# The last copy out of PSUM and the output's store on ScalarE, in a gated attention/gMLP decode kernel

## The chip, the cores and the metric

The kernel runs on one core of one Trainium2 chip. The metric is the device time of one execution in microseconds, as the median over several executions. The profile's "span" is about 1.9 us shorter than that time (385.2 against 387.0 us for the profiled execution of the kernel before) and moves with it.

## The reference

One token (batch 1, sequence 1, width 1024) goes through two branches that a sigmoid gate mixes. Branch A is attention with 32 query heads over 4 cached key/value heads of 65,536 positions; branch B is a small gMLP block. Cut to what matters:

```python
g = sigmoid((x * gate_w).sum(-1, keepdims=True))
q = (x @ wq)                                    # 32 heads of 128
p = softmax(q @ repeat(k_cache, 8).T * 128**-0.5)
a = (p @ repeat(v_cache, 8)) @ wo               # out: (1, 1, 1024), bfloat16
b = gmlp(x, w_in, w_sp, b_sp, w_out)
return g * a + (1 - g) * b
```

The caches and weights are 162 MB, the output is 2 KB.

## The kernel before

SyncE issues all large loads in program order into a ring of four 4 MB buffers. At the very end the output projection accumulates into one tile `out_ps` in PSUM, the memory that the matmuls write to; it has 128 partitions by 256 float32 columns, in which four groups of 32 equal rows hold the four quarters of the output. The last weight, `wo`, comes in ever smaller chunks, so that little work remains after the last of them. Then one copy casts the PSUM tile to bfloat16, and one DMA stores four of its rows, 512 B each.

```python
WO_SPLIT = ((16,), (8, 4, 2, 1, 1))
# ... loads, queries, 4 heads of scores, softmax and values: cut ...
    wo_view = A_wo.rearrange("(p c) n -> p c n", c=OC)
    c0 = 0
    for split in WO_SPLIT:
        t = kv.tile([P, CT * P], BF16, name="wo_t", tag="kv")
        t = t[:].rearrange("p (c n) -> p c n", n=D)
        b = c0
        for n in split:
            nc.sync.dma_start(out=t[:, c0 - b:c0 - b + n, :], in_=wo_view[:, c0:c0 + n, :])  # L417
            project(t[:, c0 - b:c0 - b + n, :], n, oa, c0, last=(c0 + n == OC))      # matmuls, L382
            c0 += n
    out_sb = const.tile([P, NO], BF16, name="out_sb")
    nc.vector.tensor_copy(out=out_sb[:], in_=out_ps[:])                              # L421
    nc.sync.dma_start(out=out.rearrange("o t (q n) -> (o t q) n", n=NO), in_=out_sb[::B, :])  # L422
```

## Time and profile before

| | before |
|---|---|
| time, median of 3 (range) | 386.87 us (386.82 to 386.92) |
| span of the profiled execution | 385.2 us |
| read from HBM | 162.01 MB, 421 GB/s over the span |
| from the end of the last matmul to the end of the span | 3.00 us |

Lines of the page of the kernel before. PE is TensorE and PEld its weight loads, DVE is VectorE, ACT ScalarE, POOL GpSimd. First the title and the busy time of each engine with its share of the span; then the share of busy time in 40 equal slices, in tenths, for ScalarE (ACT) and for the DMA engines; then the DMA queues with packets, MB and share of the 16 engines' time; last the chain that ended last, by engine.

```profile
span 385.2 us, 3265 instructions
PE 212.4 (55%) x1396; PEld 89.7 (23%) x1396; DVE 209.2 (54%) x207; ACT 39.2 (10%) x54; POOL 4.4 (1%) x10
...
ACT  1010001111601101014011010140110101400000
...
DMA  8999999999999999999999999999999999999993
...
q1 hardware_dynamic: 6200, 162.01, 98.1%
...
q10 hardware_dynamic: 36, 0.00, 0.0%
...
DMA 65%; DVE 18%; PE 9%; issue 5%; ACT 1%; SPq 0%; ACTq 0%; DVEq 0%
```

The DMA row stands at 9 from the second slice to the last but one, and SyncE's load queue q1 is busy for 98.1% of the span: the kernel is bound by its input stream. No compute engine is over 55%. At the end only the last slice (3) falls off: in it lies the tail, by which I mean the stretch from the end of the last matmul to the end of the span. ScalarE has nothing in the last five slices. Its queue q10 carries only 36 packets, the four tiny loads at the start.

The tail itself, as the timeline of the kernel before from 381 us (start, length, engine, line, operation, and in brackets how long the engine was idle and what ended it; SPq is SyncE's issuing of a DMA):

```profile
381.12 0.29 PE L382 MATMUL out_ps<-wo_t,oa 128*32 128x256 bf16 x4 [0.25 <-DMA wo_t<-in_A_wo_dram]
...
381.76 0.41 PE L382 MATMUL out_ps<-wo_t,oa 128*32 128x256 bf16 x4 [0.35 <-DMA wo_t<-in_A_wo_dram]
...
382.22 0.42 DVE L421 CAST out_sb<-out_ps 128x256 bf16<-128x256 f32 x1 [12.43 <-PE out_ps L382]
382.67 0.66 SPq L422 DMA_DIRECT2D out_dram<-out_sb  x1
```

Read it as a staircase: each step starts where the one above it ends. The last chunk releases the last four matmuls at 381.76, they release the copy at 382.22, the copy releases the store's issue at 382.67, which ends at 383.33. The rest up to 385.17 is the store's flight (until its data packets move), its landing, and the closing steps of the program. Nothing else is going on, so all of this should be on the critical path; the 32 copies below test it.

What SyncE itself waits for at the end (longest in total first: waiter, what released it, total us, times, longest):

```profile
SPq L422 <- DVE out_sb L421: 30.3, 1, 30.3
...
SPq L457 <- DMA out_dram<-out_sb: 0.7, 1, 0.7
```

With its last load issued, it waited for VectorE's copy for the last 30.3 us before the store; no load is queued behind the store. L457 is the program's close, whose last wait is for the store's landing.

### The profile page before, as it was taken

The page shows a single profiled execution, that of the slowest core. Times are in us where ns is not written, and L with a number is a line of the kernel's source. Part 1 is how long each engine was busy: PE and PEld are TensorE (multiplying, and loading weights), DVE is VectorE, ACT ScalarE, POOL GpSimd, SP SyncE. Part 2 cuts the span into 40 slices and gives each one's busy share as a digit, 9 for nine tenths or more (in the row PEclk, how much of TensorE's full clock was granted, in tenths as well). Part 3 has the DMA queues.
Part 4 walks back from the last instruction along what each step waited for, and adds up shares of the span by engine and source line. Part 5 has one row for each costly group of instructions (what it writes and reads, how often), then busy time and mean ns, then how long its engine had stood idle before and what let it go on. Part 6 is the DMA issues. An engine that isn't in the chain of part 4 may idle for free.

```text
span 385.2 us, 3265 instructions
## 1 busy us (share of the span) xinstructions
PE 212.4 (55%) x1396; PEld 89.7 (23%) x1396; DVE 209.2 (54%) x207; ACT 39.2 (10%) x54; POOL 4.4 (1%) x10
## 2 busy tenths in 40 slices
PE   0433447775377656464876474637773837663352
PEld 0111113232222212122322121222221312331141
DVE  5141288996697372757864636569646456510010
ACT  1010001111601101014011010140110101400000
POOL 4000000000000000000000000000000000000000
PEclk9966559999779969695699695977895958565558
DMA  8999999999999999999999999999999999999993
GB/s 334 429 436 434 436 433 432 436 431 435 432 429 427 429 419 434 432 432 436 434 436 429 434 429 433 422 436 427 425 432 430 436 436 436 427 429 430 427 408 149
DMA packets 6251, 162.23 MB, mean 421 GB/s; under 512 B 728, under 2 KB 732, under 8 KB 1116
## 3 DMA queue, kind: packets, MB, share of 16 engines
q1 hardware_dynamic: 6200, 162.01, 98.1%
q8 instruction: 11, 0.18, 0.2%
q14 instruction: 4, 0.03, 0.0%
q10 hardware_dynamic: 36, 0.00, 0.0%
HBM read 162.01 MB, written 0.00 MB: 421 GB/s over the span
## 4 chain that ended last, share of the span: by engine, by line
DMA 65%; DVE 18%; PE 9%; issue 5%; ACT 1%; SPq 0%; ACTq 0%; DVEq 0%
DMA kn<-in_A_k_cache_dram 44%; DVE kt L295 15%; DMA vt<-in_A_v_cache_dram 9%; DMA wo_t<-in_A_wo_dram 9%; PE s_ps L301 6%; DMA wb<-in_B_b_sp_dram 2%; DVE pt L335 1%; PE o_ps L344 1%; PE z_ps L190 1%; ACT sc L310 1%; PE om_ps L355 0%; SPq L417 0%; ACT sc L332 0%; DVE mx L314 0%; DVE mx L297 0%
## 5 line engine op out<-in xcount | busy, mean ns | idle before, releaser
L301 PE MATMUL s_ps<-kt,wt 128*128 128x512 bf16 x512 | 139.0, 426 | 88.4 <-DVE kt L295 87.2
L295 DVE STREAM_TRANSPOSE kt<-kn 128x2048 int32<-128x2048 int32 x64 | 143.3, 2283 | 68.4 <-DMA kn<-in_A_k_cache_dram 68.4
L301 PEld LDWEIGHTS <-wt 128*128 128x128 bf16 x512 | 52.6, 105 | 173.5 <-DVE kt L295 72.8
L344 PE MATMUL o_ps<-vt,pt 128*32 128x512 bf16 x512 | 39.4, 457 | 15.4 <-DMA vt<-in_A_v_cache_dram 15.4
L310 ACT CAST sc<-s_ps 128x1024 bf16<-128x1024 f32 x16 | 16.2, 1013 | 254.9 <-PE s_ps L301 254.9
L344 PEld LDWEIGHTS <-pt 128*32 128x32 bf16 x512 | 15.9, 109 | 34.9 <-issue 27.1
L335 DVE STREAM_TRANSPOSE pt<-sc 128x1024 bf16<-128x1024 bf16 x16 | 18.6, 1217 | 6.8 <-ACT sc L332 6.8
L332 ACT ACTIVATE sc<-sc,nb 128x1024 bf16<-128x1024 bf16 x16 | 18.2, 1136 | 9.5 <-DVE nb L328 9.5
L352 DVE COPY o_sb<-o_ps 128x512 f32<-128x512 f32 x4 | 2.6, 662 | 27.2 <-PE o_ps L344 27.2
L297 DVE TENSOR_REDUCE mx<-sc 128x1 f32<-128x1024 bf16 x12 | 14.3, 1188 | 1.2 <-ACT sc L310 1.1
L355 PE MATMUL om_ps<-o_sb,pick 128*32 128x128 f32 x32 | 7.7, 421 | 13.1 <-DVE o_sb L352 13.1
L190 PE MATMUL q_ps<-wq_t,xT 128*32 128x512 bf16 x64 | 7.1, 623 | 9.1 <-DMA wq_t<-in_A_wq_dram 9.1
L314 DVE TENSOR_REDUCE mx<-sc 128x1 f32<-128x1024 bf16 x4 | 4.9, 1220 | 12.3 <-ACT sc L310 12.3
L382 PE MATMUL out_ps<-wo_t,oa 128*32 128x256 bf16 x128 | 6.0, 334 | 7.7 <-DMA wo_t<-in_A_wo_dram 7.7
L190 PEld LDWEIGHTS <-xT 128*32 128x32 bf16 x128 | 5.2, 140 | 20.5 <-issue 20.5
L355 PEld LDWEIGHTS om_ps<-o_sb,pick 128*32 128x32 f32 x32 | 5.0, 168 | 17.2 <-DVE o_sb L352 16.3
L254 DVE TENSOR_TENSOR rowt<-q_ps,own_b 128x512 f32<-128x512 f32 x2 | 1.3, 685 | 14.1 <-PE q_ps L190 14.1
L190 PE MATMUL z_ps<-win_t,xT 128*32 128x448 bf16 x64 | 6.2, 567 | 4.8 <-DMA win_t<-in_B_w_in_dram 4.8
L421 DVE CAST out_sb<-out_ps 128x256 bf16<-128x256 f32 x1 | 0.4, 425 | 12.4 <-PE out_ps L382 12.4
L318 PE MATMUL mt_ps<-ident_f,m 128*1 128x128 f32 x4 | 1.2, 296 | 10.2 <-DVE m L316 10.2
L382 PEld LDWEIGHTS <-oa 128*32 128x32 bf16 x128 | 4.4, 116 | 9.1 <-issue 7.2
L202 DVE TENSOR_TENSOR rowt<-z_ps,own_b 128x448 f32<-128x448 f32 x2 | 1.2, 620 | 9.3 <-PE z_ps L190 9.3
(86 smaller groups left out, 57.4 us busy)
## 6 DMA issues: line engine op xcount, KB each, us to landing
kn<-in_A_k_cache_dram SPq DMA_DIRECT2D x16, 4096.0 KB, 27.1
vt<-in_A_v_cache_dram SPq DMA_DIRECT2D x16, 4096.0 KB, 34.6
wq_t<-in_A_wq_dram SPq DMA_DIRECT2D x2, 4096.0 KB, 28.3
win_t<-in_B_w_in_dram SPq DMA_DIRECT2D x2, 3584.0 KB, 15.0
wo_t<-in_A_wo_dram SPq DMA_DIRECT2D x1, 4096.0 KB, 31.1
wout_t<-in_B_w_out_dram SPq DMA_DIRECT2D x1, 3584.0 KB
wo_t<-in_A_wo_dram SPq DMA_DIRECT2D x1, 2048.0 KB
wo_t<-in_A_wo_dram SPq DMA_DIRECT2D x1, 1024.0 KB
```

The source lines that it names most:

```text
L190: nc.tensor.matmul(ps[t * B:(t + 1) * B, k * HN:k * HN + n], lhsT=xT[:, i * KH + c:i * KH + c + 1].to_broadcast([P, B]), rhs=w[:, c, o:o + ...
L295: nc.vector.transpose(out=kt[:].bitcast(I32), in_=kb[:, v * n:(v + 1) * n])
L297: nc.vector.reduce_max(**late.pop())
L301: nc.tensor.matmul(s_ps[:, k * HN:(k + 1) * HN], lhsT=wt[g % 2][:, v, b].rearrange("p a v h -> p (a v h)"), rhs=kx[:, b // 2, b % 2, k * C ...
L310: nc.scalar.copy(out=sct[g, j][:], in_=s_ps[:])
L314: nc.vector.reduce_max(**late.pop())
L332: nc.scalar.activation(out=sct[g, j][:], in_=sct[g, j][:], func=ACT.Exp, scale=SCALE, bias=nb[:, 0:1], accum_out=lss[g][:, j:j + 1])
L335: nc.vector.transpose(out=ptt[g, j][:].rearrange("p c x -> p (c x)"), in_=sct[g, j][:])
L344: nc.tensor.matmul(o_ps[g][t * B:(t + 1) * B, :], lhsT=ptt[g, j][:, c, :], rhs=vx[:, c], start=(j == 0 and c < NB), stop=(j == NT - 1 and ...
L352: nc.vector.tensor_copy(out=o_sb[:], in_=o_ps[g][:])
L355: nc.tensor.matmul(om_ps[gs, :], lhsT=pick[:, i * REP:(i + 1) * REP, :].rearrange("p h q -> p (h q)"), rhs=o_sb[:, i * DH:(i + 1) * DH], s ...
L382: nc.tensor.matmul(out_ps[t * B:(t + 1) * B, :], lhsT=vec[:, c0 + c:c0 + c + 1].to_broadcast([P, B]), rhs=w[:, c, t * NO:(t + 1) * NO], st ...
```

## The change

The intent is to have one engine do copy and store, without a hand-over from VectorE to SyncE, on ScalarE, which is idle at the end.

```diff
     out_sb = const.tile([P, NO], BF16, name="out_sb")
-    nc.vector.tensor_copy(out=out_sb[:], in_=out_ps[:])
-    nc.sync.dma_start(out=out.rearrange("o t (q n) -> (o t q) n", n=NO), in_=out_sb[::B, :])
+    nc.scalar.copy(out=out_sb[:], in_=out_ps[:])
+    nc.scalar.dma_start(out=out.rearrange("o t (q n) -> (o t q) n", n=NO), in_=out_sb[::B, :])
```

## The prediction

> **What bounds the kernel now.** The input stream. The page gives 162.01 MB read at 421 GB/s over a span of 385.2 us, the load queue busy 98.1% of the span, and the DMA row at 9 in all slices but the first and last. The chain that ended last is 65% DMA; VectorE's 18% and TensorE's 9% of it are the handshakes inside that stream. The change edits only the tail behind the last weight chunk, which is wholly on the critical path.
>
> **The tail before** (timeline from 381 us, span's clock): the last wo_t chunk lands at 381.72; the last out_ps matmuls end near 382.19; VectorE's copy L421 starts about 0.05 us later and takes 0.425 us; SyncE starts issuing the store about 0.03 us after its end, at 382.67, and takes 0.66 us; the rest up to 385.2 (1.84 us) is the store's flight, its landing and the closing barrier.
>
> **What changes.** In instruction order one copy leaves VectorE, one DMA leaves SyncE, and both stand at the end of ScalarE's list; nothing else moves. No activation-table load is added: the op is the same plain copy as the L310 casts, which run between exponentials without a reload.
>
> Term by term:
> 1. Start of the copy after TensorE: L310 casts on ScalarE start 0.036 us after the last matmul's end, L421 on VectorE 0.048 us after it: -0.01 us.
> 2. The copy: L310 takes 1013 ns for 1024 columns. With the 0.833 ns per element of the Trainium skill's "ScalarE: Activation LUTs" (What ACT_TABLE_LOAD costs), 256 columns make an estimated 1013 - 768 x 0.833 = 373 ns, against 425 ns on VectorE: -0.05 us.
> 3. Copy to issue: 0.03 us across engines now. On ScalarE the DMA is still made to wait for the copy's semaphore, so I expect 0.03 to 0.1 us: 0 to +0.07 us.
> 4. The issue itself: the store takes 658 ns on SyncE, where the loads take 328 to 437 ns. ScalarE's four issues at the start took 593, 283, 277 and 274 ns; the first looks cold. ScalarE's next DMA comes 380 us later: cold again, 0.55 to 0.75 us; 0.3 us would be the lucky case: about 0 us, -0.35 at best.
> 5. Flight and landing: unchanged. The Trainium skill's "DMA: Bandwidth & Descriptors" (Issuing engines are not separate DMA queues) says that transfers from either engine end on the same 16 DMA engines, and that another issuer saves only sequencer time. The load queue is empty by then, so there is nothing to overtake: 0.
> 6. VectorE and SyncE are freed of work, but only after everything else: worth nothing. SyncE's last closing wait is still for this store.
>
> **Sum:** -0.06 us, with -0.4 to +0.3 as the plausible spread, on 386.87. Predicted 386.8 us, 8 in 10 between 386.4 and 387.2. This is "same": 98%; faster by 2% would need 7.7 us, more than the whole tail of 3.4 us.
>
> **What would show it.** Everything up to 382.2 us agrees between the profiles; L421 is on ACT at about 0.37 us; the store stands under ACTq with 0.55 to 0.75 us, and its 4 data packets of 512 B on q10 instead of q1; no added ACT_TABLE_LOAD; VectorE's instruction count falls by one.
>
> **What would make it wrong.** A table load before the copy (+1.28 us, as at the start); a wake-up or cold fetch of ScalarE after 50 us without work; a slower issue for stores on ScalarE; or another chip or clock state shifting both kernels by more than the edit.

## The result and the profile after

| | before | after |
|---|---|---|
| time, median of 4 | 386.89 us (386.82 to 387.11) | 387.04 us (386.67 to 387.11) |
| ratio after/before | | 1.0001, interval 0.9984 to 1.0018 |
| span of the profiled execution | 385.17 us | 385.24 us |

A ratio here is the mean time of one kernel's runs over that of the other's of the same rounds, so it is not quite the ratio of the medians quoted beside it. A later timing of the kernel after with five runs gave 386.82 us against 386.84.

Of the page of the kernel after, the lines that answer to those shown of before:

```profile
span 385.2 us, 3265 instructions
PE 213.5 (55%) x1396; PEld 90.3 (23%) x1396; DVE 208.7 (54%) x206; ACT 39.6 (10%) x55; POOL 4.4 (1%) x10
...
ACT  1010001111601101014011010140110101400000
...
DMA  8999999999999999999999999999999999999993
...
q1 hardware_dynamic: 6192, 162.01, 98.1%
...
q10 hardware_dynamic: 44, 0.01, 0.0%
...
DMA 68%; DVE 19%; issue 6%; PE 5%; ACT 1%; SPq 1%; DVEq 0%; ACTq 0%
```

The instruction counts moved by one (DVE 207 to 206, ACT 54 to 55) and eight packets moved from q1 to q10: the store's four rows and four small ones. The shares of the chain shift by a few points between PE and DMA. An edit at the end did not cause that: a second profile of the unchanged kernel (`before_again`, below) has DMA 58% and PE 16%. The two rows shown are the same.

The tail after, from the same timeline:

```profile
380.76 0.89 PE L382 MATMUL out_ps<-wo_t,oa 128*32 128x256 bf16 x8
...
381.89 0.41 PE L382 MATMUL out_ps<-wo_t,oa 128*32 128x256 bf16 x4 [0.24 <-DMA wo_t<-in_A_wo_dram]
...
382.34 0.37 ACT L421 CAST out_sb<-out_ps 128x256 bf16<-128x256 f32 x1 [49.44 <-PE out_ps L382]
382.74 0.61 ACTq L422 DMA_DIRECT2D out_dram<-out_sb  x1
```

It is the same staircase with two steps on another engine. The last matmuls start 0.13 us later than before (381.89 against 381.76), because in this execution the stream ended that much later; the staircase from there on is a little shorter. And the waits of SyncE at the close:

```profile
SPq L457 <- DMA wo_t<-in_A_wo_dram: 33.0, 4, 30.6
...
SPq L457 <- DMA out_dram<-out_sb: 2.5, 1, 2.5
```

SyncE now goes through its closing waits early, with the last loads, and then waits 2.5 us instead of 0.7 us for the store. It is freed of work, and gains nothing by it: the store's landing is still what it waits for last.

The trace's records of instructions and DMA packets, in nanoseconds, split the tail further. The profiler models the ends of matmuls, so the first row is less certain than the others; it is 47 or 48 ns throughout. Each column is one profiled execution; the rows add up to the tail. The two last columns are the two half changes described below.

| ns | before | after | copy on ScalarE only | store on ScalarE only |
|---|---|---|---|---|
| last matmul's end to the copy's start | 48 | 47 | 47 | 48 |
| the copy | 425 | 372 | 372 | 423 |
| copy's end to the store's issue | 28 | 30 | 25 | 32 |
| issue | 658 | 611 | 658 | 613 |
| issue's end to the first data packet | 588 | 634 | 589 | 635 |
| first packet to the last packet's end | 99 | 99 | 99 | 97 |
| last packet's end to SyncE's seeing the landing | 344 | 338 | 342 | 338 |
| from there to the end of the span | 808 | 814 | 807 | 814 |
| **tail** | **2998** | **2945** | **2939** | **3000** |

### The profile page after: what moved, and what is told of

It reads as the page before. It is cut to its first block, busy times and chain, and to the rows that moved or that the text cites. A ratio compares the mean times of both kernels' runs of the same rounds, so it can differ in the third digit from the quotient of the medians.

```text
span 385.2 us, 3265 instructions
## 1 busy us (share of the span) xinstructions
PE 213.5 (55%) x1396; PEld 90.3 (23%) x1396; DVE 208.7 (54%) x206; ACT 39.6 (10%) x55; POOL 4.4 (1%) x10
## 4 chain that ended last, share of the span: by engine, by line
DMA 68%; DVE 19%; issue 6%; PE 5%; ACT 1%; SPq 1%; DVEq 0%; ACTq 0%
DMA kn<-in_A_k_cache_dram 45%; DVE kt L295 17%; DMA vt<-in_A_v_cache_dram 9%; DMA wo_t<-in_A_wo_dram 9%; DMA win_t<-in_B_w_in_dram 5%; PE s_ps L301 2%; PE o_ps L344 1%; DVE pt L335 1%; PE z_ps L190 1%; ACT sc L310 1%; PE om_ps L355 0%; SPq L417 0%; ACT sc L332 0%; DVE mx L314 0%; DVE mx L297 0%
## 5 line engine op out<-in xcount | busy, mean ns | idle before, releaser
L301 PE MATMUL s_ps<-kt,wt 128*128 128x512 bf16 x512 | 137.4, 421 | 89.7 <-DVE kt L295 89.5
L310 ACT CAST sc<-s_ps 128x1024 bf16<-128x1024 f32 x16 | 16.2, 1013 | 254.5 <-PE s_ps L301 254.5
L297 DVE TENSOR_REDUCE mx<-sc 128x1 f32<-128x1024 bf16 x12 | 14.2, 1187 | 0.9 <-ACT sc L310 0.8
L382 PE MATMUL out_ps<-wo_t,oa 128*32 128x256 bf16 x128 | 8.0, 414 | 5.7 <-DMA wo_t<-in_A_wo_dram 5.7
L382 PEld LDWEIGHTS <-oa 128*32 128x32 bf16 x128 | 5.4, 137 | 8.1 <-issue 5.8
```

The costliest lines, as they stand in the source:

```text
L297: nc.vector.reduce_max(**late.pop())
L301: nc.tensor.matmul(s_ps[:, k * HN:(k + 1) * HN], lhsT=wt[g % 2][:, v, b].rearrange("p a v h -> p (a v h)"), rhs=kx[:, b // 2, b % 2, k * C ...
L310: nc.scalar.copy(out=sct[g, j][:], in_=s_ps[:])
L382: nc.tensor.matmul(out_ps[t * B:(t + 1) * B, :], lhsT=vec[:, c0 + c:c0 + c + 1].to_broadcast([P, B]), rhs=w[:, c, t * NO:(t + 1) * NO], st ...
```

## The experiments

Theory A: the tail is a serial sum, wholly on the critical path, and the change altered one term of it, the length of the copy, by 0.05 us; that is below what the time can show. Rivals: (B) one engine doing both shortens the tail by a saved hand-over; (C) the store's issue is cold and its length is what counts; the tail is absorbed by something else; the issuer of the store matters; the change has an effect on the stream.

### The two halves of the change

The edit of the first, `copy_only`:

```diff
-    nc.vector.tensor_copy(out=out_sb[:], in_=out_ps[:])
+    nc.scalar.copy(out=out_sb[:], in_=out_ps[:])
     nc.sync.dma_start(...)
```

> Half of the change: ScalarE copies, SyncE still stores. Theory A (the tail behind the last matmul is a serial sum and only the copy's length changed): from the end of the last out_ps matmul to the end of the span 2.94 us as in the kernel after, against 3.00 before, all 0.05 us of it in the copy (372 against 425 ns). Theory B (one engine doing both is what shortens the tail, by saving a hand-over between engines): 3.00 us or more, because the hand-over to SyncE is back. Either way the measured time stays within 0.5 us of before, since the end of the input stream varies by 0.1 us and more from run to run.

The edit of the second, `store_only`:

```diff
     nc.vector.tensor_copy(out=out_sb[:], in_=out_ps[:])
-    nc.sync.dma_start(...)
+    nc.scalar.dma_start(...)
```

> The other half: VectorE copies, ScalarE stores. Theory A: tail 3.00 us as before, the copy 425 ns, hand-over about 0.03 us, ScalarE's issue about 0.6 us and about 1.25 us from the start of the issue to the first data packet. Theory B: longer than 3.00 us, by the hand-over from VectorE to ScalarE. Measured time within 0.5 us of before.

Measured, five runs each beside nine of the kernel before (387.06 us): `copy_only` 386.91 us, ratio 0.9998 (0.9986 to 1.0011); `store_only` 386.82 us, ratio 0.9999 (0.9986 to 1.0012). The times cannot tell the halves apart; the tails in the table above can. With the copy alone on ScalarE the tail is 2939 ns, as short as with both; with the store alone there it is 3000 ns, as long as before. In timelines, first of `copy_only`:

```profile
382.30 0.37 ACT L421 CAST out_sb<-out_ps 128x256 bf16<-128x256 f32 x1 [49.35 <-PE out_ps L382]
382.70 0.66 SPq L422 DMA_DIRECT2D out_dram<-out_sb  x1
```

and of `store_only`:

```profile
382.19 0.42 DVE L421 CAST out_sb<-out_ps 128x256 bf16<-128x256 f32 x1 [13.48 <-PE out_ps L382]
382.65 0.61 ACTq L422 DMA_DIRECT2D out_dram<-out_sb  x1
```

Two things follow. The hand-over costs the same within one engine as between two: 30 ns from ScalarE to itself, 25, 28 and 32 ns for the three pairs of different engines. Theory B falls. And ScalarE's issue is 45 ns shorter than SyncE's, but the first packet then comes 46 ns later after the end of it: from the start of the issue it is 1246, 1245, 1247 and 1248 ns in the four kernels. Between the two engines, the shorter issue is no gain.

### The copy, 32 times

The edit of `copies_dve` in the kernel before; `copies_act` has the same loop around `nc.scalar.copy` in the kernel after. The result stays right.

```diff
-    nc.vector.tensor_copy(out=out_sb[:], in_=out_ps[:])
+    for _ in range(32):
+        nc.vector.tensor_copy(out=out_sb[:], in_=out_ps[:])
```

> The kernel before with its final copy done 32 times over, the same values (the result stays right). If the tail is wholly on the critical path, 31 more copies of 425 ns or somewhat less where they overlap lengthen the time by 8 to 13.5 us. If the tail is absorbed by something else that ends later (a fixed close, a slower transfer), the time grows by less than the copies' own span.

> The kernel after with its final copy done 32 times over. Theory A: it grows by 31 of ScalarE's copies, 8 to 11.5 us, and is faster than the 32 copies on VectorE by 31 times the difference of one, so by about 0.05 x 32 = 1.7 us if the copies do not overlap; this lifts the 0.05 us of the change out of the noise. Rival (the copy is equal in cost on both, or a repeated copy shows another ratio): under 0.5 us apart, or VectorE faster.

Measured: 401.24 us on VectorE (400.91 to 401.28), 399.30 us on ScalarE (399.14 to 399.44), 386.96 us for the kernel before beside them. The kernel after was not timed in these rounds, so both growths are counted from the kernel before. Timeline of `copies_dve`:

```profile
381.96 14.63 DVE L422 CAST out_sb<-out_ps 128x256 bf16<-128x256 f32 x32 [13.41 <-PE out_ps L382]
396.62 0.66 SPq L423 DMA_DIRECT2D out_dram<-out_sb  x1
```

and of `copies_act`:

```profile
382.11 12.88 ACT L422 CAST out_sb<-out_ps 128x256 bf16<-128x256 f32 x32 [48.90 <-PE out_ps L382]
395.02 0.61 ACTq L423 DMA_DIRECT2D out_dram<-out_sb  x1
```

Each row is all 32 copies, from the first one's start to the last one's end. One copy more costs 458 ns on VectorE (424 for the copy, 34 between it and the next) and 403 ns on ScalarE (372 and 31). 31 x 458 ns is 14.2 us, and the time grew by 14.3 us: nothing absorbs the tail. 31 x 403 ns is 12.5 us, and the time grew by 12.3 us. My ranges for both (8 to 13.5 and 8 to 11.5 us) were too low, since I had allowed for overlap of the copies, and there is none. The two kernels differ by 1.94 us in the time, against 1.7 us expected; their tails in the traces differ by 1.76 us. This lifts the 0.05 us of the change out of the noise, and it has the sign and size that the single copy shows.

### A chain of eight DMAs of the store's form

The edit of `hops_sp` in the kernel before; `hops_act` has `nc.scalar` in the kernel after.

```diff
     nc.vector.tensor_copy(out=out_sb[:], in_=out_ps[:])
+    hops = [const.tile([P, NO], BF16, name=f"hop{i}") for i in range(8)]
+    for h in hops:
+        nc.sync.dma_start(out=h[::B, :], in_=out_sb[::B, :])
+        out_sb = h
     nc.sync.dma_start(out=..., in_=out_sb[::B, :])
```

> The kernel before, with a chain of 8 DMAs of the store's form (4 rows of 512 B, tile to tile) put between copy and store, all issued by SyncE, each waiting for the one before. Each hop costs issue, flight and landing, about 1.7 us if like the store: +12 to 16 us. If the issue is cold only once, issues after the first fall to 0.3 to 0.45 us, and by the time from issue to first packet of the later hops one sees whether flight counts from the start or the end of the issue.

> The same chain in the kernel after, all issued by ScalarE. Theory A (issuer does not matter): within 0.5 us of the chain on SyncE for 9 DMAs, so within 0.05 us for one. Rival (the issuer matters): a difference of 0.1 us or more per DMA, over 0.9 us in all.

Measured: 399.26 us with SyncE, 399.43 us with ScalarE, 386.96 us for the kernel before. Timeline of `hops_sp`:

```profile
382.48 0.64 SPq L424 DMA_DIRECT2D hop<-out_sb  x1
384.16 9.72 SPq L424 DMA_DIRECT2D hop<-hop  x7
394.92 0.54 SPq L426 DMA_DIRECT2D out_dram<-hop  x1
```

and of `hops_act`:

```profile
382.72 0.59 ACTq L424 DMA_DIRECT2D hop<-out_sb  x1
384.41 9.87 ACTq L424 DMA_DIRECT2D hop<-hop  x7
395.33 0.55 ACTq L426 DMA_DIRECT2D out_dram<-hop  x1
```

From the second hop's start to the store's start are seven steps: 10.76 us, 1.54 us each, on SyncE; 10.92 us, 1.56 us each, on ScalarE. ScalarE is slower by 0.02 us per DMA, far from the 0.1 us that the rival asked for. The first issue of the chain is the longest on both (641 and 588 ns), "cold" in what follows; the later ones, "warm", take 493 to 506 and 513 or 514 ns, not the 0.3 to 0.45 us that I expected. The store at the end of the chain takes 537 and 553 ns. So most of the store's long issue remains when it is warm. Whether that comes from the form, from a source in SBUF (the on-chip memory of the tiles) or from the wait ahead of each hop, these runs do not separate: ScalarE's first two loads of the program, of one form and without such a wait, took 593 and 283 ns.

A warm DMA also gets its first packet sooner: 1129 to 1142 ns after the start of its issue on SyncE, 1157 or 1158 on ScalarE, against 1238 and 1225 for the first. For a hop, coldness is thus worth about 0.1 us on SyncE and 0.07 us on ScalarE; for the store itself, whose first packet comes 1175 and 1198 ns after the start of its issue here and 1246 and 1245 ns without the chain, 0.07 and 0.05 us.

The chain was also to show whether flight counts from the start or the end of the issue. On ScalarE it is the end: in all its DMAs of this form, cold or warm, the first packet comes 634 to 645 ns after the end of the issue, but 1157 to 1253 ns after its start. Warm DMAs on SyncE have 632 to 643 ns from the end; only the cold ones there have less, 588 to 597. So what the half changes compared was SyncE's cold issue, some 45 ns longer than ScalarE's without a later packet.

Nor do the runs say what makes an issue cold. The cold DMAs were both the first of their form and came after the longest pauses (33 us or more on SyncE, 378 us or more on ScalarE); SyncE's 4 MB loads after waits of up to 15 us took 328 ns.

### A dummy DMA ahead of the store

These two runs were to see whether the issue is cold: `warm_act` has ScalarE issue a DMA of the same form ahead of the store. It reads the weight chunk before the last, so that it waits for that chunk. `warm_sp` does the same on SyncE in the kernel before.

```diff
             nc.sync.dma_start(out=t[:, c0 - b:c0 - b + n, :], in_=wo_view[:, c0:c0 + n, :])
+            if c0 == OC - 2:
+                pre = const.tile([P, NO], BF16, name="pre")
+                nc.scalar.dma_start(out=pre[::B, :], in_=t[::B, c0 - b, :NO])   # warm_sp: nc.sync
             project(t[:, c0 - b:c0 - b + n, :], n, oa, c0, last=(c0 + n == OC))
```

> The kernel after, plus a dummy DMA of the same form (4 rows of 512 B, from the weight chunk before the last into a spare tile) that ScalarE issues about 1 us ahead of the store. Theory C (the 611 ns of ScalarE's issue are a cold issue, as its first one of the program at 612 ns against 269 to 329 for the next three): the store's issue falls to about 0.3 us, and if flight counts from the end of the issue (634 ns to the first packet) the tail falls from 2.94 to about 2.6 us. Theory D (a store of this form takes 0.6 us whatever came before, or flight counts from the issue's start at 1.25 us): the tail stays at 2.94 us, even if the issue gets shorter. Measured time: C -0.3 us, D within 0.3 us of before.

> The same dummy DMA in the kernel before, issued by SyncE. Theory C: the store's issue on SyncE falls from 658 ns to 0.33 to 0.44 us as its loads took, and the tail from 3.00 to about 2.7 us. Theory D: 658 ns or the 1246 ns from issue start to first packet stay, tail 3.00 us. If only one of the two engines gains by it, the issuer does matter when warm.

Measured, beside the kernel before at 387.06 us: `warm_act` 386.76 us, ratio 0.9996 (0.9983 to 1.0008); `warm_sp` 389.83 us, ratio 1.0073 (1.0060 to 1.0087). Neither did what Theory C said, for two different reasons.

The timeline of `warm_act`:

```profile
380.92 0.59 ACTq L420 DMA_DIRECT2D pre<-wo_t  x1
...
382.04 0.37 ACT L424 CAST out_sb<-out_ps 128x256 bf16<-128x256 f32 x1 [49.05 <-PE out_ps L382]
382.44 0.55 ACTq L425 DMA_DIRECT2D out_dram<-out_sb  x1
```

In `warm_act` the store's issue fell from 611 only to 547 ns, and the first packet came 1190 instead of 1245 ns after its start. That is 55 ns gained. But the tail is 2989 ns, 44 more than in the kernel after. SyncE's wait for the store ends at 384.07 us, 0.91 us before the end of the span, where in the kernel after that is 0.79 us (both from the end of the wait's record; the table counts from its start): two further closing waits stand behind it in the list, each some 60 ns, where the store's was the last before. With one DMA more, the store's place in that list is another one. So a gain of 55 ns was lost to two closing waits that now came behind the store's.

In `warm_sp` my experiment was flawed. Timeline:

```profile
381.13 0.64 SPq L420 DMA_DIRECT2D pre<-wo_t  x1
...
381.84 0.37 SPq L417 DMA_DIRECT2D wo_t<-in_A_wo_dram  x1
384.61 0.41 PE L382 MATMUL out_ps<-wo_t,oa 128*32 128x256 bf16 x4 [3.05 <-DMA wo_t<-in_A_wo_dram]
...
385.06 0.42 DVE L424 CAST out_sb<-out_ps 128x256 bf16<-128x256 f32 x1 [16.30 <-PE out_ps L382]
385.51 0.56 SPq L425 DMA_DIRECT2D out_dram<-out_sb  x1
```

The dummy stands in SyncE's list before the last load of `wo`, and it waits for the chunk ahead of that. SyncE works through its list in order, so the last load was not issued until 381.84 us, when in the kernel before its data had all come by 381.28 us, and the last matmuls waited 3.05 us for it. The same DMA with the same wait on ScalarE, in `warm_act`, held up nothing. By the 2% rule `warm_sp` still counts as "same", but its interval leaves no doubt that it is slower. This is a case, made by accident, in which the issuer of a small DMA matters: with a load behind it the DMA cost 2.8 us against the kernel before, and on the other engine nothing that the time shows. In the kernel before none stand behind the store. Its own tail (3051 ns, with the issue at 563 ns and the first packet at 1195 ns) repeats what `warm_act` shows: a gain of about 50 ns up to the first packet, and more than that lost at the close.

### The control

> Control: the kernel before, unchanged, timed against itself. Ratio 1.000 with an interval of about 0.1% either way; this is how much two equal programs differ. In the profile the tail from the last out_ps matmul to the end is 3.00 us again, within 0.01 us, while the end of the last load moves by 0.1 us or more against the first profile.

> The kernel after, unchanged, beside the control. Theory A: ratio 0.9999 (0.05 of 387), which cannot be told from the control; in the profile the tail is 2.945 us within 0.01 us. If the change had an effect on the stream ahead of the tail (other lanes or queues for the loads, other instruction fetches), the ratio would leave the control's interval.

Measured, five runs each beside nine of the kernel before (386.84 us): `before_again` 386.95 us, ratio 1.0001 (0.9987 to 1.0015); `after_again` 386.82 us, ratio 1.0000 (0.9987 to 1.0012). The change lies within the interval that a kernel has against itself. Their tails are 2995 and 2954 ns, so over six profiles the tail is 2995, 2998 and 3000 ns with VectorE's copy and 2939, 2945 and 2954 ns with ScalarE's, while the last packet of the loads ended at 381.27 to 381.48 us in the one group and at 381.29 to 381.41 us in the other. The stream's end varies four times as much as the change is worth, and shows no sign of the change.

## Why the prediction was right

The prediction of 386.8 us (386.4 to 387.2), "same" at 98%, held: 387.04 us in the first timing, 386.82 us in the second. The time could hardly have refuted it, since it cannot show 0.05 us; whether the terms were right is for the traces to say. By these terms:

1. *Start of the copy, -0.01 us.* There was no gain: 47 against 48 ns. The 36 ns of ScalarE's other copies were taken behind other matmuls and did not carry over.
2. *The copy, -0.05 us.* Right: 373 ns estimated, 372 measured, 425 before. The slope of 0.833 ns per element in the Trainium skill's "ScalarE: Activation LUTs" (What ACT_TABLE_LOAD costs) agrees: (1013 - 372) ns over 768 columns is 0.835. No table load was added, as the count of ScalarE's instructions shows (54 to 55).
3. *Copy to issue, 0 to +0.07 us.* Right, at the low end: 30 against 28 ns. Sharing an engine saves no hand-over.
4. *The issue, about 0 us.* 611 ns lies in the predicted 0.55 to 0.75 us. The range held in part by luck: I took most of the length for coldness, but the chains show 0.05 to 0.1 us of that, and the rest stays when the DMA is warm. (The loads' issues, too, ranged up to 500 ns in the kernel before, not 437.) Whether my "lucky" 0.3 us would have brought the -0.35 us no run shows: the 45 ns between the two engines' issues never reached the first packet, while the 64 ns that `warm_act` took off ScalarE's own issue brought it 55 ns sooner.
5. *Flight and landing, 0.* Right in sum, 1245 against 1246 ns from the issue's start to the first packet. The Trainium skill's "DMA: Bandwidth & Descriptors" (Issuing engines are not separate DMA queues) says of DMAs issued from several engines at once that this only saves the sequencer's time to initiate them, which is not quite this case of one DMA on another engine; here even the 47 ns saved in the issue were not saved in the whole.
6. *VectorE and SyncE freed: worth nothing.* Right; SyncE merely waits longer for the store at the close.

The sum of -0.06 us compares with -53 ns between the first two profiles. One sign that I had named was wrong: everything up to 382.2 us was to agree between the profiles, and the stream ended 0.13 us later in the one of after. The control shows that to be the stream's own variation. It is also enough to account for the first medians, which went the wrong way by 0.15 us.

What stays open: why a cold DMA of this form costs 0.05 to 0.1 us more, and why the flight makes up for the difference between the two engines' cold issues; the runs show both, and not their cause.

The Trainium skill's "Perfetto Trace Analysis" (DMA Instruction — HWDGE (DVE, Sync)) has a reading for the second: the issue that a profile shows also contains the sequencer's own semaphore increments, which come after the descriptors are generated, so its end need not be where flight begins. That the store's first packet keeps its distance from the issue's start (1245 to 1253 ns in six profiles) and not from its end (588 to 636 ns) would agree with it. The chains limit that: on ScalarE, cold or warm, it is the distance from the end that stays (634 to 645 ns). So the reading could apply at most to the extra 45 ns of SyncE's cold issue, and no run takes the issue apart.

## What to carry to other kernels

Before moving the last steps of a kernel to another engine, write the tail as a sum of terms from the trace, since only the terms that differ can pay; here that was 53 ns of a copy, and neither the hand-over nor the issuer. Here an engine that did two steps in a row still waited for its own first step, about as long as another engine did (30 ns against 25 to 32). Where a small DMA's issuer does matter is in a queue with loads behind it: a wait placed ahead of one load there cost 2.8 us.

## What the Trainium skill lacked or had wrong

- "VectorE: DVE Perf Modes", the table of PSUM-to-SBUF cycles under the TRN2 errata: for 256 float32 columns, with its factor Accel taken as 1, an estimate from it is (172 + 256)/1.2 = 357 ns on ScalarE and (120 + 256)/0.96 = 392 ns on VectorE; measured were 372 and 425 ns. It ranks them rightly, and both are too low.
- "DMA: Bandwidth & Descriptors", Latency and other measured facts, gives about 600 ns for the first byte of a DMA issued by SyncE or ScalarE, and does not say from when. Counted from the end of the issue, the trace has 588 to 636 ns for the cold store in six profiles and 632 to 645 ns for warm DMAs of its form; counted from its start, 1245 to 1253 ns and 1129 to 1198 ns.
- No page I read gives the whole length of an issue, as a profile shows it, on these two engines on trn2. Here it was 328 ns for most 4 MB loads, 493 to 514 ns for a warm DMA of four 512 B rows from tile to tile and 537 to 563 ns for one to the output, and 587 to 662 ns for a cold one.
- No page I read gives the hand-over within one engine beside that between two: 30 ns from ScalarE's copy to its own DMA, 25 to 32 ns between different engines.
